# First tile of stage one multiplied k by k, with w1 loaded by rows, shared copies and fewer warm-up matmuls

## The chip, the cores and the metric

The kernel runs on one core of one Trainium2 chip. The metric is device time in microseconds (us), the median of several executions.

## The reference

The reference adds three things: the input, an attention with a recurrent memory (part A), and a two-stage mixer and MLP (part B). Only the start of part B is touched:

```
xn = layernorm(x)                       # 2048 rows of 1024
h  = gelu(layernorm(xn) @ w1)           # w1: 1024 x 1024; "stage one" below
hs = shifted(h) @ w2                    # "phase two" below
x1 = xn + hs;  B = x1 + gelu(layernorm(x1) @ w3) @ w4
out = x + A(xn, ...) + B
```

## The kernel before

The rows are cut into 16 tiles of 128. For the first tiles VectorE computes mean and variance (`norm_stats`) and normalises (`norm2`), TensorE transposes the 128 x 1024 tile in two halves of four 128 x 128 blocks (`transposes`, as matmuls with the identity), and a copy brings each half from PSUM (where TensorE's results arrive) to SBUF (from where it reads) as bf16. Stage one then multiplies w1 with the transposed tile. There are eight output groups `co`, each a sum over eight blocks `k`. Tiles 0 to 3 go one by one (128 columns), later ones in pairs (256 columns). While it waits for the first tile, TensorE multiplies zeros, to be at full clock when work arrives. In the parts shown here, "..." marks cuts.

```python
load_x(0)
for c in range(4):                       # w1 by quarters of its columns: runs of 512 bytes
    nc.sync.dma_start(w1_sb[:, :, c * 256:(c + 1) * 256], w1_v[:, :, c * 256:(c + 1) * 256])
    if c == 1:
        load_x(1)
for n in range(2, 7):
    load_x(n)
...
def transposes(xn2, xn2T, jj, half, on_dve=False):
    ps = psum0.tile([P, 4, P], F32, tag="tr")
    for k in range(4):
        nc.tensor.matmul(ps[:, k, :], xn2[:, (half * 4 + k) * P:(half * 4 + k + 1) * P], ident[:], ...)
    if on_dve:
        nc.vector.tensor_copy(xn2T[:, jj, half * 4:half * 4 + 4, :], ps[:])
    else:
        nc.scalar.copy(xn2T[:, jj, half * 4:half * 4 + 4, :], ps[:])

def stage1(n0, nt, xn2T, between, j0=0):
    for co in range(KT):
        ps = psum.tile([P, 512], F32, tag="mm", bufs=4)
        for k in range(KT):
            nc.tensor.matmul(ps..., w1_sb[:, k, co * P:(co + 1) * P], xn2T[:, j0:j0 + nt, k, :],
                             start=(k == 0), stop=(k == KT - 1))
        nc.scalar.activation(hTB[:, co, ...], ps[:, :w], ACTF.Gelu_apprx_tanh)
        for f in between.get(co, ()):    # the next tile's transposes, between two groups
            f()
...
for i in range(15):                      # warm-up on zeros
    nc.tensor.matmul(ps[:], wz[:, :P], wz[:], start=(i == 0), stop=(i == 14))
norm_stats(0)
norm2_of(0)
tr(0, 0)
tr(0, 1, True)
norm_stats(1)
...
        if n < 4:
            stage1(n - 1, 1, ..., {5: [lambda n=n: tr(n, 0)], 6: [lambda n=n: tr(n, 1)]}, (n - 1) % 2)
```

Of the kernel before, what the change touches and what calls it, by code (L numbers as in the profile page):

```python
# [16 lines left out]
F32 = mybir.dt.float32  # L17
I32 = mybir.dt.int32
ALU = mybir.AluOpType
ACTF = mybir.ActivationFunctionType  # L20
# [3 lines left out]
P = 128  # L24
S = 2048
D = 1024
KT = D // P
# [50 lines left out]
def kernel(  # L78
# [16 lines left out]
    nc = tc.nc  # L95
# [6 lines left out]
    w1_v = B_w1.rearrange("(k p) n -> p k n", p=P)  # L102
# [90 lines left out]
    with tc.manual_schedule(engines={mybir.EngineType.PE, mybir.EngineType.SP, mybir.EngineType.Pool}), ExitStack() as actx:  # L193
# [5 lines left out]
        psum = actx.enter_context(tc.tile_pool(name="psum", bufs=4, space=PSUM))  # L199
        with ExitStack() as bctx:  # L200
# [13 lines left out]
            with ExitStack() as hctx:  # L214
                psum0 = hctx.enter_context(tc.tile_pool(name="psum0", bufs=2, space=PSUM))
                keep = hctx.enter_context(tc.tile_pool(name="keep12", bufs=1))
                hTB = keep.tile([P, KT, S + 4], BF16)
# [4 lines left out]
                with ExitStack() as p0:  # L222
                    big = p0.enter_context(tc.tile_pool(name="p0big", bufs=1))
                    ring = p0.enter_context(tc.tile_pool(name="p0ring", bufs=3))
                    w1_sb = big.tile([P, KT, D], BF16)
# [4 lines left out]
                    def load_x(n):  # L230
                        if n < NT:
                            xts[n] = ring.tile([P, D], BF16, tag="xt", bufs=10, name=f"xt{n}")
                            nc.sync.dma_start(xts[n][:], x_v[:, n, :])

                    load_x(0)
                    for c in range(4):
                        nc.sync.dma_start(w1_sb[:, :, c * 256:(c + 1) * 256], w1_v[:, :, c * 256:(c + 1) * 256])
                        if c == 1:
                            load_x(1)
                    for n in range(2, 7):  # L240
                        load_x(n)
# [7 lines left out]
                    def norm_stats(n, part=None):  # L249

                        if n >= NT:
                            return
                        xt = xts[n]
                        if n not in stats:
                            stats[n] = [ring.tile(shape, F32, tag=tag, bufs=6, name=f"{tag}{n}") for tag, shape in (("st", [P, 2, 6]), ("mv", [P, 2]), ("ab", [P, 2]), ("rr", [P, 2]), ("nm2", [P, 1]))]
                        st, mv, ab, rr, nm2 = stats[n]
                        if part in (None, 0):
                            nc.vector.bn_stats(st[:, 0, :], xt[:, 0:512])
                        if part == 0:
                            return  # L260
                        nc.vector.bn_stats(st[:, 1, :], xt[:, 512:1024])
                        nc.vector.bn_aggr(mv[:], st[:])
                        nc.vector.scalar_tensor_tensor(ab[:], epsm[:], mv[:, 1:2], epsa[:], op0=ALU.mult, op1=ALU.add)
                        nc.gpsimd.tensor_tensor(rr[:], ab[:], neghalf[:], op=ALU.pow)
                        if n >= NPE:
                            nc.gpsimd.tensor_scalar(nm2[:], mv[:, 0:1], rr[:, 1:2], -1.0, op0=ALU.mult, op1=ALU.mult)

                    def norm2(n, xn2T, jj):
                        st, mv, ab, rr, nm2 = stats[n]
                        xn2 = ring.tile([P, D], BF16, tag="xn2")  # L270
                        if n < NPE:
                            for c in (slice(0, 512), slice(512, 1024)) if n == 0 else (slice(0, 1024),):
                                nc.vector.tensor_scalar(xn2[:, c], xts[n][:, c], mv[:, 0:1], rr[:, 1:2], op0=ALU.subtract, op1=ALU.mult)
                        else:
                            nc.scalar.activation(xn2[:], xts[n][:], ACTF.Identity, bias=nm2[:], scale=rr[:, 1:2])
                            nc.sync.dma_start_transpose(xn2T[:, jj], xn2[:])
                        return xn2

                    def norm1(n):
                        st, mv, ab, rr, nm2 = stats[n]  # L280
                        xn = xn_keep[n // 4][:, n % 4]
                        nc.vector.tensor_scalar(xn, xts[n][:], mv[:, 0:1], rr[:, 0:1], op0=ALU.subtract, op1=ALU.mult)
                        nc.gpsimd.dma_start(xn_v[:, n, :], xn)
                        load_x(n + 10)
                        if n in (12, 15):
                            load_w3()
                        return xn

                    def transposes(xn2, xn2T, jj, half, on_dve=False):
                        ps = psum0.tile([P, 4, P], F32, tag="tr")  # L290
                        for k in range(4):
                            nc.tensor.matmul(ps[:, k, :], xn2[:, (half * 4 + k) * P:(half * 4 + k + 1) * P], ident[:], start=True, stop=True)
                        if on_dve:
                            nc.vector.tensor_copy(xn2T[:, jj, half * 4:half * 4 + 4, :], ps[:])
                        else:
                            nc.scalar.copy(xn2T[:, jj, half * 4:half * 4 + 4, :], ps[:])

                    def stage1(n0, nt, xn2T, between, j0=0):
                        w = nt * P
# [3 lines that stand above are left out]
                                nc.tensor.matmul(ps[:, :w].rearrange("p (n t) -> p n t", t=P), w1_sb[:, k, co * P:(co + 1) * P],  # L303
                                                 xn2T[:, j0:j0 + nt, k, :], start=(k == 0), stop=(k == KT - 1))
                            nc.scalar.activation(hTB[:, co, 2 + n0 * P:2 + n0 * P + w], ps[:, :w], ACTF.Gelu_apprx_tanh)
                            for f in between.get(co, ()):
                                f()

                    def xn2T_tile():
                        return ring.tile([P, 2, KT, P], BF16, tag="xn2T", name="xn2T")  # L310


                    wz = big.tile([P, 512], BF16)
# [2 lines left out]
                    nc.scalar.activation(gtab[:], ones_f[:], ACTF.Gelu_apprx_tanh)  # L316

                    ps = psum.tile([P, 512], F32, tag="mm", bufs=4, name="warm")
                    for i in range(15):
                        nc.tensor.matmul(ps[:], wz[:, :P], wz[:], start=(i == 0), stop=(i == 14))  # L320
                    tiles2, xn2s = {}, {}

                    def norm2_of(n):
                        if n % 2 == 0:
                            tiles2[n] = xn2T_tile()
                        xn2s[n] = norm2(n, tiles2[n - n % 2], n % 2)

                    def tr(n, half, on_dve=False):
                        transposes(xn2s[n], tiles2[n - n % 2], n % 2, half, on_dve)

                    norm_stats(0)
                    norm2_of(0)
                    tr(0, 0)
                    tr(0, 1, True)
                    norm_stats(1)
                    nc.gpsimd.memset(hTB[:, :, 0:2], 0.0)
                    nc.gpsimd.memset(hTB[:, :, S + 2:S + 4], 0.0)
                    load_consts(4)
                    for n in range(1, NPE):
                        if n > 1:  # L340
                            norm_stats(n + 1, 0)
                        norm2_of(n)
                        norm_stats(n + 1, 1 if n > 1 else None)
                        if n > 1:
                            norm1(n - 2)
                        if n < 4:
                            stage1(n - 1, 1, tiles2[(n - 1) // 2 * 2], {5: [lambda n=n: tr(n, 0)], 6: [lambda n=n: tr(n, 1)]}, (n - 1) % 2)
                    stage1(3, 1, tiles2[2], {4: [lambda: tr(4, 0)], 5: [lambda: tr(4, 1)], 6: [lambda: tr(5, 0)], 7: [lambda: tr(5, 1)]}, 1)

                    def prep(n):  # L350
# [17 lines left out]
                with ExitStack() as p2:  # L368
                    ring = p2.enter_context(tc.tile_pool(name="p2ring", bufs=4))
                    for n in range(NT):  # L370
                        x1 = ring.tile([P, D], F32, tag="x1")
                        st = ring.tile([P, 2, 6], F32, tag="st")
                        for ch in range(2):
                            ps = psum.tile([P, 512], F32, tag="mm", bufs=4)
# [20 lines left out]
            with ExitStack() as p3:  # L395
# [118 lines left out]
                for tb in range(4):  # L514
                    depth = 1 if tb < 2 else 2
                    for f in range(FT):
                        ps = psum.tile([P, 512], F32, tag="mm", bufs=4)
# [15 lines left out]
                    for j in range(4):  # L533
                        n = tb * 4 + j
# [7 lines left out]
                        for ch in range(2):  # L542
                            ps = psum.tile([P, 512], F32, tag="mm", bufs=4)
# [21 lines left out]
            for hg in range(8):  # L565
# [6 lines left out]
                for m4 in range(4):  # L572
                    Vs = vsp.tile([P, 4, 512], BF16, tag="Vs")
                    for j in range(4):
                        ps = psum.tile([P, 512], F32, tag="mm", bufs=4)
# [255 lines left out]
        for i in range(2):  # L831
            ps = psum.tile([P, 512], F32, tag="mm", bufs=4)
# [34 lines left out]
    with tc.If(cond > 0):  # L867
        with ExitStack() as fctx:
# [18 lines left out]
            with tc.For_i(0, NSEG, 1) as i:  # L887
# [6 lines left out]
                for hg in range(8):  # L894
# [8 lines left out]
                    ps = fps.tile([P, 4, L], F32, tag="mm")  # L903
# [4 lines left out]
                    ps = fps.tile([P, 4, L], F32, tag="mm")  # L908
# [4 lines left out]
                    ps = fps.tile([P, 512], F32, tag="mm")  # L913
# [33 lines left out]
                for ch in range(2):  # L947
                    ps = fps.tile([P, 512], F32, tag="op")
# [47 lines left out]
```

## Time and profile before

| | before |
|---|---|
| median time, 3 runs | 1521.8 us (1521.3 to 1522.15) |
| span of the profiled run | 1519.6 us |
| TensorE (PE) busy | 1508.8 us, 99% |
| first matmul of stage one | 8.38 us |
| first 256-column matmul of stage one (called the landmark below) | 26.35 us |
| first matmul of phase two | 69.56 us |

In the views, PE is TensorE, PEld its weight loads, DVE VectorE, ACT ScalarE, POOL GpSimd and SPq the queue of SyncE; L303 is line 303 of the kernel. The first lines are from the page of the kernel before: busy time by engine, and the shares of the chain of work that ended last.

```profile
span 1519.6 us, 24277 instructions
...
PE 1508.8 (99%) x9781; PEld 808.3 (53%) x9853; DVE 546.2 (36%) x1137; ACT 506.7 (33%) x1147; POOL 179.4 (12%) x248
...
PE 98%; DMA 1%; issue 0%; DVE 0%; ACT 0%; SPq 0%; POOL 0%
```

The next lines are PE's waits in the whole kernel before: who waited for whom, us in total, times, longest.

```profile
PE warm L320 <- DVE wz L314: 1.4, 1, 1.4
PE ps L303 <- ACT xn2T L296: 0.5, 1, 0.5
PE psO L690 <- DMA PT<-Pn: 0.4, 1, 0.4
PE ps L292 <- DVE xn L273: 0.4, 1, 0.4
PE ps L651 <- DMA wt<-in_A_Wq_dram: 0.3, 1, 0.3
PE pso L709 <- issue: 0.2, 1, 0.2
```

A kernel that is almost always busy on PE can only lose useless PE time. Three of the six lines lie in the first 12 us. The warm-up is counted as busy, though it computes nothing. The timeline of PE before shows this stretch. Its columns are start, duration, engine, line, operation, tiles, shape and count, with the idle time before and what ended it in brackets.

```profile
1.38 6.10 PE L320 MATMUL warm<-wz 128*128 128x512 bf16 x15 [1.38 <-DVE wz L314]
7.32 0.61 PE L292 MATMUL ps<-c_ident_sb,xn 128*128 128x128 bf16 x8
8.38 2.98 PE L303 MATMUL ps<-xn2T,w_sb 128*128 128x128 bf16 x48 [0.45 <-ACT xn2T L296]
11.77 0.40 PE L292 MATMUL ps<-c_ident_sb,xn 128*128 128x128 bf16 x4 [0.41 <-DVE xn L273]
12.06 0.62 PE L303 MATMUL ps<-xn2T,w_sb 128*128 128x128 bf16 x8
12.51 0.39 PE L292 MATMUL ps<-c_ident_sb,xn 128*128 128x128 bf16 x4
12.74 3.45 PE L303 MATMUL ps<-xn2T,w_sb 128*128 128x128 bf16 x56
16.03 0.39 PE L292 MATMUL ps<-c_ident_sb,xn 128*128 128x128 bf16 x4
...
26.35 2.14 PE L303 MATMUL ps<-xn2T,w_sb 128*128 128x256 bf16 x16
```

By 11.77 us PE has done 56 matmuls of use, worth 3.1 us. Matmuls of 128 columns follow each other every 0.0558 us (eight in 0.446 us). So the 72 matmuls from 11.77 to 16.03 need 4.02 us, and took 4.26. The next 72, up to the transposes of tile 3 at 20.21, took 4.18. No idle time is shown in brackets, but some 0.2 us is lost in each tile.

### The profile page before, as it was taken

Reading aid. Unit: us, or ns where it says so; the run is one execution under the profiler, and the core shown is the slowest. Engines: PE = TensorE matmul, PEld = TensorE weight load, DVE = VectorE, ACT = ScalarE, POOL = GpSimd, SP = SyncE. Lnnn points to the kernel's source line nnn. Section 1 sums busy time; section 2 is a strip of 40 time slices with the busy share of each in tenths; the row PEclk is TensorE's granted clock in tenths of the full one; section 3 lists DMA queues with packets and bytes.
Section 4 is the critical chain, followed back from the end, with each engine's and each line's share of the span. In section 5 each row is a group of like instructions: output and inputs, shape, how many; then the busy total and the mean of one; then the engine's idle time right before and its main releaser. Section 6 shows DMA issues by size and latency. Waiting matters only on the chain.

```text
span 1519.6 us, 24277 instructions
## 1 busy us (share of the span) xinstructions
PE 1508.8 (99%) x9781; PEld 808.3 (53%) x9853; DVE 546.2 (36%) x1137; ACT 506.7 (33%) x1147; POOL 179.4 (12%) x248
## 2 busy tenths in 40 slices
PE   9999999999999999999999999999999999999998
PEld 7844444445444444444466645654665555445555
DVE  7382230100120122222246614651664266416542
ACT  6533203013022011111256614650663266326630
POOL 5231020211111231100000010001000100010001
PEclk9999999999999999999999999999999999999999
DMA  8799762353355887532499947992997389628611
GB/s 283 157 266 317 220 174 93 136 201 111 126 169 141 198 281 255 192 133 70 137 240 253 238 117 189 244 238 79 228 240 190 118 223 217 185 76 209 175 46 53
DMA packets 306459, 274.20 MB, mean 180 GB/s; under 512 B 153787, under 2 KB 274128, under 8 KB 306088
## 3 DMA queue, kind: packets, MB, share of 16 engines
q1 hardware_dynamic: 284168, 189.92, 49.3%
q0 software_dynamic: 22032, 82.63, 15.9%
q8 instruction: 79, 1.29, 0.4%
q14 instruction: 36, 0.29, 0.1%
q10 hardware_dynamic: 144, 0.07, 0.0%
HBM read 190.98 MB, written 46.19 MB: 156 GB/s over the span
## 4 chain that ended last, share of the span: by engine, by line
PE 98%; DMA 1%; issue 0%; DVE 0%; ACT 0%; SPq 0%; POOL 0%
PE ps L651 30%; PE pso L709 14%; PE ps L577 14%; PE ps L519 13%; PE ps L545 13%; PE ps L377 4%; PE ps L303 3%; PE psS L666 2%; PE psO L690 2%; PE ps L836 1%; PE ps L469 1%; PE ps L434 0%; PE gps L448 0%; DMA wt<-in_A_Wq_dram 0%; DMA PT<-Pn 0%; PE warm L320 0%
## 5 line engine op out<-in xcount | busy, mean ns | idle before, releaser
L651 PE MATMUL ps<-hTb,wt 128*128 128x396 bf16 (+3 forms) x2528 | 500.4, 343 | 0.3 <-DMA wt<-in_A_Wq_dram 0.3
L651 PEld LDWEIGHTS <-wt 128*128 128x128 bf16 x2528 | 232.2, 98 | 167.6 <-DMA wt<-in_A_Wq_dram 0.7
L577 PE MATMUL ps<-wt,xT 128*128 128x512 bf16 x1003 | 220.1, 379 | 1.1
L709 PE MATMUL pso<-wo_sb,oX 128*128 128x512 bf16 x938 | 209.3, 379 | 1.2 <-issue 0.2
L519 PE MATMUL ps<-xn3T,w_sb 128*128 128x512 bf16 x896 | 196.2, 379 | 0.0
L545 PE MATMUL ps<-w_sb,h3T 128*128 128x512 bf16 x873 | 194.3, 379 | 1.2
L577 PEld LDWEIGHTS <-xT 128*128 128x128 bf16 x1024 | 100.2, 98 | 120.8
L520 ACT ACTIVATE h3T<-ps 128x512 bf16<-128x512 f32 x112 | 66.9, 597 | 290.4 <-PE ps L519 289.5
L709 PEld LDWEIGHTS <-oX 128*128 128x128 bf16 x960 | 92.6, 98 | 108.2
L657 ACT CAST KT<-ps 128x396 bf16<-128x396 f32 (+3 forms) x160 | 82.3, 514 | 186.9 <-PE ps L651 184.2
L545 PEld LDWEIGHTS <-h3T 128*128 128x128 bf16 x896 | 87.0, 98 | 103.4
L519 PEld LDWEIGHTS <-w_sb 128*128 128x128 bf16 x896 | 86.6, 98 | 102.1
L672 DVE TENSOR_REDUCE sums<-sm 99x4 f32<-99x396 f32 (+2 forms) x176 | 97.6, 555 | 113.0 <-ACT sm L670 113.0
L659 ACT ACTIVATE QT<-ps 128x396 bf16<-128x396 f32 (+3 forms) x160 | 84.2, 527 | 119.1 <-PE ps L651 102.0
L668 DVE TENSOR_TENSOR sm<-psS,c_mask_reg_sb 99x396 f32<-99x396 f32 x160 | 91.3, 571 | 86.3 <-PE psS L666 85.7
L579 ACT CAST Vs<-ps 128x512 bf16<-128x512 f32 x64 | 37.5, 587 | 233.1 <-PE ps L577 174.9
L670 ACT ACTIVATE sm<-sm 99x396 f32<-99x396 f32 (+2 forms) x176 | 92.9, 528 | 63.7 <-DVE sm L668 60.7
L583 DVE CAST Vs<-ps 128x512 bf16<-128x512 f32 x64 | 44.3, 692 | 170.0 <-PE ps L577 158.0
L678 DVE TENSOR_TENSOR Pn<-sm,rs 99x396 bf16<-99x396 f32 (+2 forms) x176 | 99.0, 562 | 7.2 <-DMA PT<-Pn 1.1
L546 DVE TENSOR_TENSOR R<-ps,R 128x512 f32<-128x512 f32 x32 | 21.9, 690 | 180.9 <-PE ps L545 166.6
L716 POOL DMA_DIRECT2D out_dram<-ot x30 | 16.4, 547 | 584.0 <-DVE ot L715 578.2
L715 DVE TENSOR_TENSOR ot<-pso,Rt 128x512 bf16<-128x512 f32 (+1 forms) x33 | 22.3, 676 | 172.3 <-PE pso L709 166.9
(120 smaller groups left out, 1072.0 us busy)
## 6 DMA issues: line engine op xcount, KB each, us to landing
wt<-in_A_Wq_dram SPq DMA_DIRECT2D x76, 512.0 KB
wt<-in_A_Wk_dram SPq DMA_DIRECT2D x76, 512.0 KB
wt<-in_A_Wv_dram POOLq DMA_DIRECT2D x24, 1024.0 KB, 6.5
V_scratch<-Vs SPq DMA_DIRECT2D x32, 512.0 KB
V<-V_scratch SPq DMA_DIRECT2D x32, 384.0 KB
R_scratch<-x POOLq DMA_DIRECT2D x16, 512.0 KB, 3.9
R<-R_scratch SPq DMA_DIRECT2D x16, 512.0 KB
R_scratch<-R POOLq DMA_DIRECT2D x16, 512.0 KB, 3.2
```

The source lines that it names most:

```text
L519: nc.tensor.matmul(ps[:].rearrange("p (n t) -> p n t", t=P), w3_sb[:, k, f * P:(f + 1) * P], xn3T[tb][:, :, k, :], start=(k == 0), stop=(k ...
L520: nc.scalar.activation(h3T[:, f, :], ps[:], ACTF.Gelu_apprx_tanh)
L545: nc.tensor.matmul(ps[:], h3T[:, f, j * P:(j + 1) * P], w4_sb[:, f, ch * 512:(ch + 1) * 512], start=(f == 0), stop=(f == FT - 1))
L577: nc.tensor.matmul(ps[:], xT[:, m4 * 4 + j, k, :], wv[:, k, :], start=(k == 0), stop=(k == KT - 1))
L651: nc.tensor.matmul(ps[:, :nb] if flat else ps[:, :nb].rearrange("p (t c) -> p t c", t=nt), w[:, k, hh * P:(hh + 1) * P], B["rhs"](k), star ...
L657: nc.scalar.copy(o, i)
L659: nc.scalar.mul(o, i, scale)
L668: nc.vector.tensor_tensor(sm[:T, :, :T], S3, t["mask"][:].unsqueeze(1).to_broadcast((T, 4, T)), op=ALU.add)
L670: nc.scalar.activation(e[:T, :, :T], sm[:T, :, :T], ACTF.Exp, scale=LN2)
L672: nc.vector.tensor_reduce(ss, e[:T, :, :T], axis=AX.X, op=ALU.add)
L678: nc.vector.tensor_tensor(Pn[:T, :, :T], e[:T, :, :T], rs[:T, :].unsqueeze(2).to_broadcast((T, 4, T)), op=ALU.mult)
L709: nc.tensor.matmul(self.ps[:, :self.w], self.oX[self.gl // 3][:, h, self.gl % 3 * P:(self.gl % 3 + 1) * P], wo_sb[:, h, self.cc], start=(h ...
```

## The change

It is meant to start the first real work earlier and to keep PE fed: w1 comes in whole rows (2 KB runs instead of 512 B) in the order in which a k-outer loop uses them, tile 1 is loaded earlier, the copies are halved, half of tile 1's statistics is taken earlier, three warm-up matmuls go, and the transposes of tiles 2 and 3 move one group forward. Line numbers after it: transposes L292, copies L294, L295 and L297, k-outer matmuls L307, other matmuls of stage one L317, phase two L394.

```diff
-    nc.sync.dma_start(w1_sb[:, :, c * 256:(c + 1) * 256], w1_v[:, :, c * 256:(c + 1) * 256])
-    if c == 1:
+    nc.sync.dma_start(w1_sb[:, 2 * c:2 * c + 2, :], w1_v[:, 2 * c:2 * c + 2, :])
+    if c == 0:
         load_x(1)
...
-        if on_dve:
-            nc.vector.tensor_copy(xn2T[:, jj, half * 4:half * 4 + 4, :], ps[:])
+        if shared:
+            nc.scalar.copy(xn2T[:, jj, half * 4:half * 4 + 2, :], ps[:, 0:2])
+            nc.vector.tensor_copy(xn2T[:, jj, half * 4 + 2:half * 4 + 4, :], ps[:, 2:4])
...
+    def stage1_k(xn2T):
+        pss = [psum.tile([P, 4, P], F32, tag="mm", bufs=4, name=f"ps{i}") for i in range(2)]
+        for k in range(KT):
+            if k == KT - 1:
+                tr(1, 0)
+                tr(1, 1)
+            for co in range(KT):
+                nc.tensor.matmul(pss[co // 4][:, co % 4, :], w1_sb[:, k, co * P:(co + 1) * P], xn2T[:, 0, k, :],
+                                 start=(k == 0 and co % 4 == 0), stop=(k == KT - 1), skip_group_check=True)
+        for i in range(2):
+            nc.scalar.activation(hTB[:, 4 * i:4 * i + 4, 2:2 + P], pss[i][:], ACTF.Gelu_apprx_tanh)
...
-    for i in range(15):
+    for i in range(12):                                  # warm-up, stop= adjusted
...
     norm_stats(0)
+    norm_stats(1, 0)
     norm2_of(0)
-    tr(0, 0)
+    tr(0, 0, True)
     tr(0, 1, True)
-    norm_stats(1)
+    norm_stats(1, 1)
...
-        if n < 4:
-            stage1(n - 1, 1, ..., {5: [lambda n=n: tr(n, 0)], 6: [lambda n=n: tr(n, 1)]}, (n - 1) % 2)
+        if n == 1:
+            stage1_k(tiles2[0])
+        elif n < 4:
+            stage1(n - 1, 1, ..., {4: [lambda n=n: tr(n, 0)], 5: [lambda n=n: tr(n, 1)]}, (n - 1) % 2)
```

More of the change, by code (lines that the diff above doesn't have):

```diff
@@ L287, in norm1, with transposes @@
                         return xn
-                    def transposes(xn2, xn2T, jj, half, on_dve=False):
+                    def transposes(xn2, xn2T, jj, half, shared=False):
                         ps = psum0.tile([P, 4, P], F32, tag="tr")
@@ L318 @@
                     ps = psum.tile([P, 512], F32, tag="mm", bufs=4, name="warm")
-                    for i in range(15):
-                        nc.tensor.matmul(ps[:], wz[:, :P], wz[:], start=(i == 0), stop=(i == 14))
+                    for i in range(12):
+                        nc.tensor.matmul(ps[:], wz[:, :P], wz[:], start=(i == 0), stop=(i == 11))
                     tiles2, xn2s = {}, {}
@@ L326, in norm2_of, with tr @@
                         xn2s[n] = norm2(n, tiles2[n - n % 2], n % 2)
-                    def tr(n, half, on_dve=False):
-                        transposes(xn2s[n], tiles2[n - n % 2], n % 2, half, on_dve)
+                    def tr(n, half, shared=False):
+                        transposes(xn2s[n], tiles2[n - n % 2], n % 2, half, shared)
                     norm_stats(0)
+                    norm_stats(1, 0)
                     norm2_of(0)
-                    tr(0, 0)
+                    tr(0, 0, True)
                     tr(0, 1, True)
-                    norm_stats(1)
+                    norm_stats(1, 1)
                     nc.gpsimd.memset(hTB[:, :, 0:2], 0.0)
@@ L345 @@
                             norm1(n - 2)
-                        if n < 4:
-                            stage1(n - 1, 1, tiles2[(n - 1) // 2 * 2], {5: [lambda n=n: tr(n, 0)], 6: [lambda n=n: tr(n, 1)]}, (n - 1) % 2)
+                        if n == 1:
+                            stage1_k(tiles2[0])
+                        elif n < 4:
+                            stage1(n - 1, 1, tiles2[(n - 1) // 2 * 2], {4: [lambda n=n: tr(n, 0)], 5: [lambda n=n: tr(n, 1)]}, (n - 1) % 2)
                     stage1(3, 1, tiles2[2], {4: [lambda: tr(4, 0)], 5: [lambda: tr(4, 1)], 6: [lambda: tr(5, 0)], 7: [lambda: tr(5, 1)]}, 1)
```

## The prediction

> **What bounds the kernel.** TensorE is busy for 1508.8 of 1519.6 us (page, part 1), and PE holds 98% of the chain that ended last; after the start its waits add up to about 1 us (waits view). The change touches only the first tiles of phase one, so it can win only useless PE time at the start. In the timeline of the first 12 us: 1.38 us until the zeros are written; 15 warm-up matmuls to about 7.3 us; 0.45 us before the first real matmul at 8.38, waiting for ScalarE's copy of the transposes (0.59 us); 0.41 us at 11.37, waiting for tile 1's normalised rows. Useful by 11.77 us are 56 matmuls at 0.056 us, 3.1 us: about 8.6 us are lost.
>
> **What changes, costed from the trace.**
> - Three fewer warm-ups: twelve end at 1.4 + 12 x 0.427 = 6.5 us. Tile 0's rows are ready by 6.99, so the warm-ups held the transposes up by some 0.3 us.
> - VectorE does the first half of tile 1's statistics (0.69 us) before tile 0's normalisation, in the hole where it waits for GpSimd (5.4 to 6.25). Tile 1 lands behind 256 + 512 KB at about 380 GB/s from 3.0 us: I estimate 5.7 us. The statistics end at 6.4 and delay tile 0 by 0.1 to 0.2 us; later they save 0.6 us on tile 1's chain.
> - Copies halved: a 256-column ScalarE copy costs about 0.38 us (as its 256-column activations), not 0.59, and only k = 0 and 1 are needed to start. VectorE's part waits for ScalarE's, but k = 2 comes 0.9 us later. First real matmul: about 7.7 us, not 8.38.
> - w1 by rows: 2 KB packets, which ran at about 380 GB/s, against about 300 for 512 B ones. The Trainium skill ("DMA: Bandwidth & Descriptors", Why small descriptors are slow) gives a fixed cost per packet; the rates here agree in direction. Row pairs should land before their use, and tile 2, waited for until 12.7 us before, about 1.5 us earlier.
> - k-outer: tile 1's transposes come before the last k. PE reaches them at about 10.8, the rows are ready at 10.9. Two 0.59 us copies then serialise on ScalarE, so stage one of tile 1 waits about 0.4 us for its second half, hidden before. Two 512-column Gelu of 0.6 us replace eight of 0.28.
>
> Sum: start 0.7 us earlier, waits about 0.2 us longer: net gain 0.5 to 0.9 us, all on the PE chain, and kept to the end because PE has no slack afterwards. Median 1521.0 us; 80% range 1519.9 to 1522.3. Faster by over 2% 0.005, within 2% 0.99, slower 0.005.
>
> **Right or wrong.** In the timeline after: warm-ups end near 6.5; first real matmul near 7.7; VectorE's first statistics of tile 1 start near 5.7, ahead of tile 0's normalisation; no DMA wait in the k loop; a PE wait of about 0.4 us for ScalarE's second copy near 12 us; phase two's first matmul 0.5 to 0.9 us before 69.56.
>
> **What would make it wrong.** The clock. The warm-ups ran at 0.427 us each until about 6.85 us, then at 0.21. The Trainium skill ("TensorE: Matmul & The Clock Gate", The HAM clock gate) says that full clock comes after a busy window of some 3.4 us of a free-running count. Three fewer warm-ups leave PE idle from 6.5 to about 6.9; if that spoils the window, matmuls run at half rate for up to 3.4 us more, a loss of up to 1.7 us, and the gain is gone. Also: tile 1 landing after 6.2 us, holding VectorE and tile 0 by as much; or a w1 row pair late.

## The result, and the profile after

The median is 1520.9 us (1519.64 to 1523.62, 6 runs), against 1521.55 us of the kernel before (1520.96 to 1522.35, 6 runs). The ratio is 0.9996, with a 95% interval of 0.9983 to 1.0009: the same within 2%. The times alone don't even show the sign of the change. The profile does. This is the timeline of PE after:

```profile
1.38 5.25 PE L334 MATMUL warm<-wz 128*128 128x512 bf16 x12 [1.38 <-DVE wz L328]
6.97 0.72 PE L292 MATMUL ps<-c_ident_sb,xn 128*128 128x128 bf16 x8 [0.34 <-DVE xn L273]
7.83 3.09 PE L307 MATMUL ps<-xn2T,w_sb 128*128 128x128 bf16 x48
11.20 0.62 PE L307 MATMUL ps<-xn2T,w_sb 128*128 128x128 bf16 x8 [0.28 <-DMA w_sb<-in_B_w_dram]
11.65 0.61 PE L292 MATMUL ps<-c_ident_sb,xn 128*128 128x128 bf16 x8
12.10 0.61 PE L307 MATMUL ps<-xn2T,w_sb 128*128 128x128 bf16 x8
12.71 2.66 PE L317 MATMUL ps<-xn2T,w_sb 128*128 128x128 bf16 x40
15.21 0.39 PE L292 MATMUL ps<-c_ident_sb,xn 128*128 128x128 bf16 x4
...
25.65 2.14 PE L317 MATMUL ps<-xn2T,w_sb 128*128 128x256 bf16 x16
```

The landmark is 0.70 us earlier (25.65 against 26.35), and so is phase two (68.86 against 69.56). But the line at 11.20 was not foreseen: after k = 5, PE waits for w1. The next lines are the chain of waits after, in order of time. It leads to 11.2 us not through TensorE but through the load of w1.

```profile
3.17 7.98 DMA w_sb<-in_B_w_dram
11.15 0.05 issue
11.20 0.62 PE ps L307 x8
11.82 0.24 PE ps L292 x4
12.06 0.02 issue
12.08 1.08 ACT xn2T L297 x2
```

The weight loads show the two waits for w1, before k = 4 and before k = 6 (the timeline of PEld after):

```profile
9.85 0.89 PEld L307 LDWEIGHTS <-w_sb 128*128 128x128 bf16 x16 [0.25 <-DMA w_sb<-in_B_w_dram]
11.19 0.45 PEld L307 LDWEIGHTS <-w_sb 128*128 128x128 bf16 x8 [0.45 <-DMA w_sb<-in_B_w_dram]
```

With the spacing of 0.0558 us, the gain can be split by counting matmuls. Both kernels have 56 done (8 transposes, 48 of tile 0) when the next piece starts, at 11.77 before and at 11.20 after: 0.57 us gained. From there to the first transposes of tile 2, 72 matmuls took 4.26 us before and lost 0.24; 64 took 4.01 us after and lost 0.44 (they need 3.57), so 0.20 is given back. That is the chain's ScalarE piece: two copies of tile 1's transposes end at 13.16, while PE could have gone on at about 12.77. From there on the kernel before loses 0.16 and 0.17 us in tiles 2 and 3, and the kernel after nothing: 0.33 gained. Together 0.57 - 0.20 + 0.33 = 0.70.

So there are three questions. Does the load of w1 really set the pace of tile 0 (then the earlier start is not what pays)? Is the 0.33 us due to the moved transposes? And which parts of the change carry the 0.57?

### The profile page after: what moved, and what is told of

Its sections match the earlier page's. It is cut to its first block, busy times and chain, and to the rows that moved or that the text cites. A ratio compares the mean times of both kernels' runs of the same rounds, so it can differ in the third digit from the quotient of the medians.

```text
span 1518.8 us, 24267 instructions
## 1 busy us (share of the span) xinstructions
PE 1508.2 (99%) x9778; PEld 806.7 (53%) x9850; DVE 545.9 (36%) x1138; ACT 504.8 (33%) x1142; POOL 179.1 (12%) x248
## 4 chain that ended last, share of the span: by engine, by line
PE 97%; DMA 1%; issue 0%; ACT 0%; SPq 0%; DVE 0%
PE ps L668 30%; PE pso L726 14%; PE ps L594 14%; PE ps L536 13%; PE ps L562 13%; PE ps L394 4%; PE ps L317 3%; PE psS L683 2%; PE psO L707 2%; PE ps L486 1%; PE ps L853 1%; DMA w_sb<-in_B_w_dram 1%; PE gps L465 0%; PE ps L451 0%; DMA wt<-in_A_Wq_dram 0%; DMA PT<-Pn 0%
```

## The experiments

In each run the landmark is read from PE's timeline, and the start of phase two from the chain of waits. Landings are the trace's records of completion: each of these loads has 16 completion counts, and a load has landed with the last one. "Full clock" is the trace's record of when TensorE's clock was granted in full. No experiment changes what is computed; all gave correct results.

| run | full clock | tile 1 landed | w1's last part landed | tile 2 landed | first matmul of stage one | landmark | phase two |
|---|---|---|---|---|---|---|---|
| before | 6.86 | 8.44 | 12.01 | 12.69 | 8.38 | 26.35 | 69.56 |
| before, repeated | 7.26 | 8.57 | 12.12 | 12.79 | 8.58 | 26.48 | 69.69 |
| after | 6.45 | 5.88 | 11.15 | 11.83 | 7.83 | 25.65 | 68.86 |
| after, repeated | 5.61 | 5.84 | 11.12 | 11.79 | 7.79 | 25.61 | 69.46 |
| 15 warm-ups | 6.12 | 5.82 | 10.68 | 11.35 | 7.80 | 25.18 | 68.88 |
| transposes after groups 5, 6 | 6.91 | 5.90 | 10.36 | 11.04 | 7.85 | 25.44 | 68.65 |
| 6 warm-ups | 13.12 | 7.08 | 11.13 | 11.81 | 9.24 | 28.19 | 71.40 |
| before + transposes after groups 4, 5 | 6.99 | 8.23 | 11.78 | 12.45 | 8.44 | 26.16 | 69.36 |
| columns, group by group | 6.51 | 6.35 | 11.73 | 12.40 | 8.29 | 26.10 | 69.31 |
| before + rows and k-outer | 7.00 | 5.95 | 10.78 | 11.46 | 8.45 | 26.17 | 69.38 |
| transposes before k = 6 | 6.71 | 5.97 | 10.04 | 10.72 | 7.91 | 25.19 | 68.40 |
| + both after group 5 | 4.18 | 5.98 | 10.05 | 10.73 | 7.93 | 25.21 | 68.42 |
| + statistics first | 6.62 | 6.99 | 11.04 | 11.71 | 8.94 | 25.63 | 69.16 |
| ScalarE alone copies | 6.73 | 6.85 | 10.90 | 11.57 | 7.61 | 24.83 | 68.73 |

### The changed kernel again

> The changed kernel, unaltered, to see how well the landmarks of one profile repeat. Theory (the last row pair of w1 sets the pace of tile 0): waits for w1 before k = 4 and before k = 6 as in the first profile, k = 6 at 11.2 us, phase two's first matmul at 68.86 within 0.1. Rival (those waits are a chance of one run, and the start of PE sets the pace): no wait for w1, phase two some 0.5 us earlier. Time about 1520.9.

The waits repeat (k = 6 at 11.16), and so does the landmark, 25.61. The time was 1520.91 us (5 runs) against 1521.93 (9 runs), ratio 0.9994 (0.998 to 1.0007). But phase two starts at 69.46, 0.60 later than in the first profile. The profile has the loss in one place, in the timeline of PE:

```profile
38.75 2.13 PE L317 MATMUL ps<-xn2T,w_sb 128*128 128x256 bf16 x18
41.36 22.87 PE L317 MATMUL ps<-xn2T,w_sb 128*128 128x256 bf16 x208 [0.48 <-ACT hTB L319]
```

Tiles 8 and 9 start here. They are transposed by DMA, not by PE. The profile names ScalarE's Gelu, but that Gelu had itself just waited for PE. The transposing DMA of tile 9, issued at 35.24, had its last completion at 41.22 us. PE went on 0.14 us after it. In the first profile of the same kernel it was 40.16, and PE passed without a wait. The profiles of two later runs name this DMA at the same place, and PE went on 0.14 us after its landing there too. Before the change PE came to this place at about 41.5 us (phase two's 69.56 less the 28.1 us that the later tiles take), after the landing at 40.78. The DMA is issued earlier after the change too (36.16 before, 35.28 and 35.24 after), but of its two landings after the change one came earlier than before and one later; why is open. So the gain of the start can be taken back here: PE arrives earlier, the DMA not always.

### Fifteen warm-ups again

```diff
-    for i in range(12):
+    for i in range(15):
```

> The changed kernel with its 15 warm-up matmuls back. Theory (w1's last row pair sets the pace of tile 0): the first transposes start about 7.2 us instead of 6.97 and the first real matmul about 8.05 instead of 7.83, but k = 6 still starts at 11.2, and phase two's first matmul stays at 68.86 within 0.1: the three matmuls bought nothing. Rival (my prediction's sum: the earlier start is the gain): phase two 0.2 to 0.3 us later, 69.1 to 69.2.

PE in the timeline of this run:

```profile
1.38 5.74 PE L334 MATMUL warm<-wz 128*128 128x512 bf16 x15 [1.38 <-DVE wz L328]
6.95 0.68 PE L292 MATMUL ps<-c_ident_sb,xn 128*128 128x128 bf16 x8
7.80 3.54 PE L307 MATMUL ps<-xn2T,w_sb 128*128 128x128 bf16 x56 [0.17 <-ACT xn2T L294]
11.18 0.61 PE L292 MATMUL ps<-c_ident_sb,xn 128*128 128x128 bf16 x8
```

The three extra matmuls delayed nothing: full clock came at 6.12 us in this run, and the rest of the fifteen ran twice as fast (one in 0.22 us instead of 0.43) and were over at 6.95. My number for the first real matmul (8.05) was therefore wrong, and the run doesn't test the rival on its own terms. It shows something else. By chance w1's last pair landed at 10.68 instead of 11.15, and the landmark came 0.47 us earlier. PE's timeline merges the wait into its third line, but the weight load of k = 6 still waited for w1 (the timeline of PEld):

```profile
10.72 0.45 PEld L307 LDWEIGHTS <-w_sb 128*128 128x128 bf16 x8 [0.25 <-DMA w_sb<-in_B_w_dram]
```

In both profiles of the changed kernel and in this one, k = 6 starts 0.04 to 0.05 us after that landing (11.20, 11.16, 10.72), and the landmark follows 14.45 us later. That is the theory's claim by another road: with nearly the same first matmul (7.83, 7.79, 7.80), the landing of w1 moved the landmark by as much as it moved itself. Phase two came at 68.88, as the theory said, but by luck: w1 was earlier than the theory assumed, and 0.49 us were lost at 61.7 us behind a transposing DMA.

### Transposes of tiles 2 and 3 back after groups 5 and 6

```diff
-    stage1(n - 1, 1, ..., {4: [lambda n=n: tr(n, 0)], 5: [lambda n=n: tr(n, 1)]}, ...)
+    stage1(n - 1, 1, ..., {5: [lambda n=n: tr(n, 0)], 6: [lambda n=n: tr(n, 1)]}, ...)
```

> The changed kernel with the transposes of tiles 2 and 3 back after output groups 5 and 6 instead of 4 and 5. Theory (the second half's copy, 0.59 us on ScalarE, no longer fits under one remaining group of eight matmuls, 0.45 us): the next tile's fifth matmul waits about 0.17 us in each of two tiles, phase two's first matmul at 69.2, 0.33 later than 68.86. Rival (the move only keeps order, as my prediction treated it): 68.9, no change.

The number, 69.2, failed (68.65), because w1 landed early here as well (10.36, no wait for it). The part under test can still be read apart from that. Stage one of tile 1 starts at 12.18 instead of 12.71, 0.53 earlier, but the landmark is only 0.21 earlier: 0.32 was lost in between, where 0.33 was expected. The wait is back in the timeline of PE: after the transposes of tile 2, 56 matmuls cover 3.45 us instead of 3.29.

```profile
16.01 3.45 PE L317 MATMUL ps<-xn2T,w_sb 128*128 128x128 bf16 x56
```

ScalarE's copy of a half takes 0.59 us, and one group of eight matmuls plus four of the next tile cover 0.67 us less the delays on both ends. One more group in between removes the wait.

### Six warm-ups

```diff
-    for i in range(12):
+    for i in range(6):
```

> The changed kernel with 6 warm-up matmuls. Theory (their use is the clock alone): they end about 4.0 us, PE idles for 3 us, and the transposes and tile 0's matmuls then run at about 0.107 us each until past 10 us; k = 6 comes 1.5 to 2.5 us later than 11.2 and phase two's first matmul at 70 to 71.5. Rival (the zeros are useless, and w1 sets the pace anyway): 68.86, no change.

PE in the timeline of this run, the transposes and tile 0's matmuls:

```profile
8.17 1.03 PE L292 MATMUL ps<-c_ident_sb,xn 128*128 128x128 bf16 x8 [4.05 <-DVE xn L273]
9.24 5.12 PE L307 MATMUL ps<-xn2T,w_sb 128*128 128x128 bf16 x56
```

The 56 matmuls took 5.12 us, against 3.29 us where no load held them up, since full clock came only at 13.12 us. The landmark is 28.19 and phase two 71.40. About 1.2 us of this is another accident: tile 1 landed at 7.08, and VectorE, which does tile 1's first statistics before tile 0's normalisation, held tile 0 up by as much. The rest is the clock, less the waits for w1 that it hid (0.68 us by the spacing in the changed kernel). Part of PE's idle time of 4.05 us comes from the accident, so this one run doesn't show what six would do without it. Here too few zeros cost time, and twelve are enough: in all eight profiles with twelve the full clock came between 4.18 and 6.91 us.

### One line of the change in the kernel before

```diff
-    {5: [lambda n=n: tr(n, 0)], 6: [lambda n=n: tr(n, 1)]}
+    {5 - (n > 1): [lambda n=n: tr(n, 0)], 6 - (n > 1): [lambda n=n: tr(n, 1)]}
```

> The kernel before with one line of the change alone: the transposes of tiles 2 and 3 one output group earlier. Landmark: the first 256-column matmul of stage one, at 26.35 us before and 25.65 after. Theory (the second half's copy does not fit under one group): each of the two next tiles loses its wait of 0.17 us, landmark 26.0. Rival (all of the gain is in tile 0): 26.35.

The landmark is 26.16: 0.19 and 0.32 us better than the two profiles of the kernel before. The two waits of 0.17 us are gone (72 matmuls in 4.03 and 4.02 us). Of the 0.14 that the nearer profile leaves missing, 0.07 came from tile 1's transposes (11.84 instead of 11.77). Another 0.06 was lost on the way to tile 2's, which started at 15.71: tile 2 landed at 12.45, its rows take 3.2 us more, and the moved transposes ask for them earlier. So the whole 0.33 of the changed kernel needs tile 2 to be early too.

### All of the change but the rows and the k-outer loop

```diff
-    nc.sync.dma_start(w1_sb[:, 2 * c:2 * c + 2, :], w1_v[:, 2 * c:2 * c + 2, :])
+    nc.sync.dma_start(w1_sb[:, :, c * 256:(c + 1) * 256], w1_v[:, :, c * 256:(c + 1) * 256])
...
-            stage1_k(tiles2[0])
+            stage1(0, 1, tiles2[0], {5: [lambda: tr(1, 0)], 6: [lambda: tr(1, 1)]}, 0)
```

> The changed kernel with tile 0 multiplied output group by output group again and w1 loaded by column quarters; 12 warm-ups, shared copies, split statistics and earlier transposes kept. Theory (with 512 B packets the last quarter lands at 12.0 us as before, and groups 6 and 7 need it): first real matmul about 7.9, but group 6 not before 12.0; landmark 25.9, later than 25.65, so the rows and k-outer order are worth 0.25 us or more. Rival (k-outer only adds the wait for the second copy, and the gain is the earlier start): 25.4 or earlier.

The landmark is 26.10. That is what the one line above gives alone (26.16): without the rows, the shared copies, the split statistics and the fewer zeros were worth some 0.06 us. PE in the timeline of this run shows why:

```profile
8.29 0.27 PE L317 MATMUL ps<-xn2T,w_sb 128*128 128x128 bf16 x2
8.75 2.84 PE L317 MATMUL ps<-xn2T,w_sb 128*128 128x128 bf16 x46 [0.18 <-DVE xn2T L295]
11.55 0.40 PE L292 MATMUL ps<-c_ident_sb,xn 128*128 128x128 bf16 x4
11.78 0.61 PE L317 MATMUL ps<-xn2T,w_sb 128*128 128x128 bf16 x8
```

Group by group, the third matmul already needs k = 2, VectorE's share of the copy, and waits for it (8.75). By the spacing PE loses 0.35 us there, 0.11 before k = 6 and 0.34 before tile 2's transposes at 15.65, whose rows come late (tile 2 landed at 12.40). Group 6 starts at 11.78, just after the last quarter of w1 landed at 11.73; it loses nothing there, but it could not have come earlier. In packets of 512 B the quarters land about 1.8 us apart; the row pairs of the changed kernel about 1.35.

### The rows and the k-outer loop alone, in the kernel before

```diff
+    w1 by row pairs, tile 1 after the first; stage1_k for tile 0, as in the change; nothing else
```

> The kernel before with w1 by rows, tile 1's load earlier and tile 0 multiplied k by k, and nothing else of the change: 15 warm-ups, whole copies, whole statistics of tile 1 after tile 0, transposes of tiles 2 and 3 after groups 5 and 6. Theory (the parts hang together: rows of tile 1 are ready at 11.7 us as before, so a faster w1 has nothing to feed): tile 1's transposes at 11.7, a wait of 0.4 us for the second copy, landmark (first 256-column matmul of stage one) 26.1 to 26.4, no gain on 26.35. Rival (rows and k-outer alone carry the gain that the run without them lost): 25.7.

The landmark is 26.17, 0.2 to 0.3 us better than before, far from 25.65. w1 landed at 10.78 and held nothing up; PE waited for tile 1's rows (transposes at 11.84) and then for the second copy. So neither part alone carries the gain. By the nearest profiles, the rows with the k-outer loop alone gain 0.18, everything else alone gains 0.25, and both together 0.70 although w1 held them up.

### The kernel before again

> The kernel before, unaltered, for the repeat of its landmarks. Theory (its tile 0 is paced by the rows of tile 1 and by ScalarE's copies, not by a straggling DMA): landmark 26.35 within 0.1, whatever the landing of w1's last quarter between 11.7 and 12.1. Rival (its start jitters as that of the changed kernel does): a spread of 0.3 us or more.

The landmark is 26.48, outside my 0.1 by a little: full clock came later (7.26 against 6.86), the transposes followed the warm-ups at 7.52 instead of 7.32, and the first matmul came at 8.58 instead of 8.38. The landings of w1 were alike in both profiles, so this run says little on the rival.

### Tile 1's transposes before k = 6

```diff
-            if k == KT - 1:
+            if k == KT - 2:
                 tr(1, 0)
                 tr(1, 1)
```

> The changed kernel with tile 1's transposes before the matmuls of k = 6 instead of k = 7: they fill the wait for w1's last row pair and give the two ScalarE copies 0.9 us of cover. Theory (the next limit is tile 2: its rows are ready 3.2 us after it lands): the PE wait of 0.44 us for the second copy goes, but the transposes of tile 2 wait for their rows instead; landmark 25.6 if tile 2 lands at 11.8 us, 25.15 if at 11.0. Rival (the copy wait is worth its length): 25.2 and 24.75.

The landmark is 25.19. But w1 and tile 2 landed the earliest of all runs (10.04 and 10.72), and the run with 15 warm-ups has 25.18 at landings of 10.68 and 11.35 without this edit. The wait for the copy is gone, as meant. In its place PE waits 0.42 us for tile 1's rows, at 11.17. Neither theory named that limit, and both numbers missed.

### And tile 2's transposes both after group 5

```diff
-    {4: [lambda n=n: tr(n, 0)], 5: [lambda n=n: tr(n, 1)]}
+    ({5: [lambda n=n: tr(n, 0), lambda n=n: tr(n, 1)]} if n == 2 else {4: ..., 5: ...})
```

> As the last one, and tile 2's two transposes both after output group 5, where its rows are ready and two groups cover the copies. Expected to beat both kernels by a few tenths of a microsecond in the landmark: 25.2 if tile 2 lands at 11.8 us, 24.8 if at 11.0, no PE wait between the transposes of tile 1 and of tile 2 except for tile 2's rows. Rival (nothing is left to win here): 25.65. Median time 1520.5, within the spread of the others.

The landmark is 25.21, the same as in the last run, so this number (24.8 or less at this landing of tile 2, 10.73) missed too. The reason is the same too, as PE's timeline of this run shows (the idle time in brackets):

```profile
11.18 0.62 PE L292 MATMUL ps<-c_ident_sb,xn 128*128 128x128 bf16 x8 [0.42 <-DVE xn L273]
```

The time was 1520.34 us (1519.93 to 1520.96, 5 runs) against 1521.6 (9 runs), ratio 0.9987 (0.9973 to 1.0001).

### Tile 1's statistics before VectorE's copies

```diff
     norm2_of(0)
+    norm_stats(1, 1)
     tr(0, 0, True)
     tr(0, 1, True)
-    norm_stats(1, 1)
```

> As the kernel with tile 1's transposes before k = 6 and tile 2's both after group 5, and VectorE does the second half of tile 1's statistics before its copies of tile 0's transposes, in the 0.5 us in which it waits for ScalarE. Theory (the next limit is the chain of tile 1's rows on VectorE): rows ready at about 9.8 instead of 11.1, transposes at about 10.6 without a wait, landmark 24.7 if w1 lands early (10.0), 24.9 to 25.0 if late (11.2), against 25.2 of that kernel. Rival (the later copies hold up k = 2 by as much, or w1 does): 25.2. Median time 1520.0, under both kernels.

This kernel also has the edits of the last two. Tile 1's rows no longer hold PE up: from the first real matmul on there is no wait but the last 0.17 us before the landmark, which every run has. But tile 1 landed at 6.99 in this run, with 14 of its 16 completions in by 6.0, and VectorE stood still for it, with tile 0's normalisation behind it (at 7.62). In the timeline of VectorE (DVE):

```profile
7.01 0.69 DVE L258 BATCH_NORM_STATS2 st<-xt 128x6 f32<-128x512 bf16 x1 [1.58 <-DMA xt<-in_A_x_dram]
```

The first matmul came at 8.94 instead of 7.9, and the landmark at 25.63. Had it been 1 us earlier, as in the runs where tile 1 landed at 5.9 to 6.0, the landmark would be 24.6; that is an estimate. The risk lies in the change itself: its new order on VectorE makes tile 0 depend on tile 1. The time was 1520.51 us (6 runs) against 1521.77 (11 runs), ratio 0.9991 (0.9976 to 1.0005).

### ScalarE alone copies, and tile 1's statistics come after tile 0

```diff
         if shared:
             nc.scalar.copy(xn2T[:, jj, half * 4:half * 4 + 2, :], ps[:, 0:2])
-            nc.vector.tensor_copy(xn2T[:, jj, half * 4 + 2:half * 4 + 4, :], ps[:, 2:4])
+            nc.scalar.copy(xn2T[:, jj, half * 4 + 2:half * 4 + 4, :], ps[:, 2:4])
...
     norm_stats(0)
-    norm_stats(1, 0)
     norm2_of(0)
+    norm_stats(1)
     tr(0, 0, True)
-    tr(0, 1, True)
-    norm_stats(1, 1)
+    tr(0, 1)
```

> As the kernel with tile 1's transposes before k = 6 and tile 2's both after group 5, but ScalarE alone copies tile 0's transposes (two copies of 256 columns, then one of 512), and VectorE does all of tile 1's statistics after tile 0's normalisation and before nothing of tile 0. Theory (a late landing of tile 1 then holds up tile 1 alone, and VectorE no longer waits for ScalarE): first transposes at 6.7, first real matmul at 7.5 to 7.6 whatever tile 1's landing up to 7.0, tile 1's rows at 9.8, landmark (first 256-column matmul of stage one) 24.2 if w1's last pair lands at 10.0, 24.7 to 25.0 if at 11.2. Rival (VectorE's share of the copies is needed): first real matmul as before at 7.9 or a wait at k = 2, landmark 25.2 or later. Median time 1520.0 if nothing takes the gain back later; the wait near 41 us for the transposing DMA of tile 8, seen in two runs, may take back up to 0.8.

This kernel also has the two edits of the kernel with tile 2's transposes both after group 5. Tile 1 was late again (6.85), and now it cost nothing. PE in the timeline:

```profile
6.75 0.72 PE L292 MATMUL ps<-c_ident_sb,xn 128*128 128x128 bf16 x8
7.61 3.04 PE L307 MATMUL ps<-xn2T,w_sb 128*128 128x128 bf16 x48
...
40.62 23.63 PE L317 MATMUL ps<-xn2T,w_sb 128*128 128x256 bf16 x215 [0.28 <-DMA xn2T<-xn]
```

The landmark is 24.83, between the expectation's two cases, and 1.52 us better than before. But w1's last pair, which was to decide between the cases, didn't set it: it landed at 10.90, and k = 6 followed the transposes at 10.94 without a loss. By the spacing PE lost 0.19 us before k = 4, for w1's third pair, and 0.30 us before tile 2's transposes, for their rows, which the expectation didn't name (the timeline of PEld):

```profile
14.82 0.45 PEld L292 LDWEIGHTS <-xn 128*128 128x128 bf16 x8 [0.31 <-DVE xn L273]
```

Then 0.69 is given back at tiles 8 and 9, where the transposing DMA landed at 40.49, and phase two starts at 68.73. The time was 1520.14 us (1519.14 to 1521.04, 5 runs) against 1522.22 (1520.71 to 1524.17, 9 runs), ratio 0.9983 (0.9969 to 0.9997). It is the only interval that lies wholly under 1, and still far from 2%. Of the 2 us between the medians the profile accounts for 0.8 (phase two at 68.73 against 69.56). The profiles don't show the rest; the kernel before was itself 0.3 to 0.7 us slower in this batch than in the others (1521.55 to 1521.93).

## Why the prediction was right, and where its reasons were not

The time was right: 1521.0 predicted, 1520.9 measured, "the same" at 2%. That alone says little: 1521.55, no change at all, lies in the stated range (1519.9 to 1522.3) too. Point by point:

- **PE bounds the kernel, and what is won at the start is kept.** Mostly right. After phase two has begun, the rest of the kernel takes 1449.4 to 1450.8 us in all fourteen profiles, so a gain there is kept, under a scatter as large as itself. Before that, "kept to the end because PE has no slack afterwards" failed: from the landmark to phase two it is 43.21 us in the ten undisturbed profiles, but 43.53 to 43.90 in four, all of them of changed kernels. In three of the four the time went at tiles 8 and 9 behind a transposing DMA; in the run with 15 warm-ups it went at 61.7 us, at a later one. So the forecast for phase two, 0.5 to 0.9 us before 69.56, holds in the first profile (68.86) and fails in the repeat (69.46).
- **Earlier start.** The effects came as described: warm-ups over near 6.5, tile 1's statistics at 5.90 (predicted 5.7), first real matmul 7.83 (predicted 7.7). The conclusion drawn from it was wrong. The sum took the start's 0.7 us as the gain. In both profiles of the changed kernel PE ran into the load of w1, so the start only made that wait longer.
- **"Row pairs should land before their use", "no DMA wait in the k loop".** This is the step that failed. There were waits of 0.25 and 0.45 us on the weight loads. The bytes came about as fast as estimated: at the prediction's 380 GB/s the last three pairs (1.5 MB) take 4.1 us after tile 1, due at 5.7, which gives an estimate of 9.8; 14 of the last pair's 16 completions were in by 10.3. One came at 11.15. The estimate worked with a mean rate, and a load has landed only when its slowest part has. In the ten profiles with row pairs the last pair landed anywhere from 10.04 to 11.15. Tile 2 was late with it: 0.86 us earlier than before (11.83 against 12.69), not 1.5.
- **A 0.4 us wait for ScalarE's second copy.** Right in sum: 0.44 lost, 0.20 more than before; by the spacing 0.17 of it went to the first half's copy.
- **Transposes of tiles 2 and 3 one group earlier.** Not costed at all. It is worth 0.33 us, nearly half of the net gain. So the sum came out right by luck: an omitted gain made up for an unforeseen wait.
- **The clock.** The fear didn't come true with twelve warm-ups in eight profiles, and did in the one with six.

The Trainium skill bears on the step that failed. "DMA: Bandwidth & Descriptors" (Why a DMA increments its semaphore by 16 and not by 1) says that a transfer runs on up to 16 engines that finish independently and each count the semaphore up; the completions listed here agree, since in some runs all sixteen come within 0.3 us and in others one or two come 0.7 us after the rest:

```
landing of w1's last row pair, its 16 completion counts in us from the span's start
after:              9.8 9.9 9.9 9.9 9.9 9.9 9.9 9.9 10.0 10.0 10.0 10.1 10.1 10.3 10.4 11.2
transposes at 5, 6: 9.8 9.8 9.9 9.9 9.9 10.0 10.0 10.0 10.0 10.0 10.1 10.1 10.1 10.1 10.1 10.4
before k = 6:       9.7 9.8 9.8 9.8 9.8 9.8 9.8 9.9 9.9 9.9 9.9 9.9 9.9 10.0 10.0 10.0
```

In the first of these runs the lag arose once: the last completion comes 0.02 us after the one before it for tile 1 (landed at 5.88), and 0.74 to 0.77 us after it for each of the five loads from w1's second pair (8.44) to tile 3. That fits one part that fell behind between 5.9 and 8.4 us and didn't catch up; the trace doesn't say which part a count belongs to. What makes it late in some runs stays open. No run here took a suspected cause away.

## What to carry to other kernels

Estimate a load's landing from its slowest completion over several profiles, not from a mean rate, and don't put work that is urgent (here VectorE's normalisation of tile 0) behind work that waits for a load (here tile 1's statistics). When the parts of a change are tested singly and gain little, test them together before one of them is dropped: each may wait for the same next thing. And before a gain at the start is called kept, look at the next place where PE meets a DMA whose landing need not move with the start.

## What the Trainium skill lacked or had wrong

- "DMA: Bandwidth & Descriptors" states bandwidths and a first-byte latency, but gives no figure for how far the sixteen completions of one load lie apart when many loads are queued. In these runs it was 0.3 to 1.7 us for loads of 256 and 512 KB (tile 1 with 6 warm-ups: 5.39 to 7.08), and it differed between executions of the same program (0.80 and 0.98 us for w1's last quarter in the two profiles of the kernel before).
- The same page's section on small descriptors puts the gain from larger packets down to fixed costs per packet and per descriptor, and gives no rate for loads issued from SyncE in packets of 512 B. Here column quarters of w1 (512 B) landed 1.77 us apart and row pairs (2 KB) 1.35 us apart, 512 KB each: about 300 and 390 GB/s.
- "TensorE: Matmul & The Clock Gate" says that a busy window of a free-running count brings full clock, so that the moment varies (here 4.18 to 7.26 us with 12 or 15 warm-ups, which agrees), but not how much idle time such a window may hold and still bring it. No run here settles that. With twelve warm-ups the long idle times (up to 1.6 us before the transposes) came after full clock, which stayed; with six, PE was idle for 4.05 us before it, and full clock came at 13.12 us.
